# An attention and two mixture layers under one static order: longer planner costs for three kinds of VectorE and GpSimd steps, and an undivided early load of the first expert's w1

## The chip, the cores and the metric

The kernel runs on one core of a Trainium2 chip. The metric is the time of an execution in device microseconds (us), the median of several runs. TensorE (PE), VectorE (DVE), ScalarE (ACT), GpSimd (POOL) and SyncE (SP, which issues most DMAs) each run their own queue of instructions in order.

## The reference, cut to what matters

```python
# attention: q, k, v (4, 8, 576, 64), f (4, 8, 576)
scores = scale * (q @ k.T) + cum[:, :, :, None] - cum[:, :, None, :]   # causal mask
x = softmax(scores) @ v                                                # -> (2304, 512)
# dense layer, w_in (512, 2048), w_out (2048, 512)
h = maximum(x @ w_in, 0)
x = h * h @ w_out
# routed layer: 8 experts with 288 tokens each, taken in order of the logits
logits = x @ w_gate
for idx in argsort(-logits.flatten()):
    tok, e = idx // 8, idx % 8
    if assigned[tok] < 0 and counts[e] < 288:
        assigned[tok] = e; counts[e] += 1
for e in range(8):
    out[assigned == e] = maximum(x[assigned == e] @ w1[e], 0) @ w2[e]
```

`w_in` and `w_out` arrive as 64-bit floats.

## The kernel before, in words

**Attention** (`pair`, `attention`, `att_tail`) goes over 4 batches with 4 head pairs each, 16 pairs in all. Per pair TensorE makes score products in four query blocks (L501). VectorE adds the decay row and takes the row's extremum in one step (L518, tile `st`), ScalarE takes the exponential (L525), TensorE transposes (L557), ScalarE or VectorE evict (L385, L389), and TensorE multiplies with v (L574). Before a block's scores are reduced, the causal mask is added into its decay row (L513, VectorE or GpSimd). `norm_rows` (L604 to L616) inverts the sums, `norm` (L623) scales the output, which goes to DRAM (`xd`).

**Conversion** (`w_piece`, L653 to L657): each of 32 pieces of `w_in` and `w_out` comes as pairs of 32-bit words. Three VectorE steps make a 32-bit float `a`, then ScalarE or GpSimd round it to `hi`, and VectorE or GpSimd subtract (`lo`, L657).

**Dense layer**: chunks of 256 tokens (`moe1_x`, `moe1_up`, `moe1_down`). An up block is 12 products (L693 to L695: hi*hi, lo*hi, hi*lo), followed by ReLU, square, `hh` and `hl` (L710); a down block is three products (L717 to L719). `x2_rows` stores results to DRAM (`x2d`). On VectorE `gate_weights` (L850, L853) folds `w_out` with the gate matrix, and `x2_sums` (L798) makes logits of four chunks. Both read `wgb`, the gate matrix broadcast to all partitions, whose space is free only when attention is over.

**Routing and experts**: `phase(m)` finds by histograms which expert fills next and who its tokens are; `expert(m)` loads the expert's number into a register of SyncE (L1192), loads w1 and w2 with it (L1204, L1218), gathers tokens from `x2d` (`xg`, L1185), transposes (L1252), multiplies (L1272 or L1276 to L1278, L1301 or L1304 to L1306), and scatters (L1324). Experts 0 to 4 take their weights unsplit, 5 to 7 split into hi and lo. The weights lie in the slots `z0` to `z31` of the dense weights, most of which also hold the last two chunks' `h` tiles (`h2`).

**The order** is a plan. Each step is recorded with the engines that can do it and a cost in ns for each (`s.op({"dve": ..., "pool": ...}, ...)`), and with tiles it reads and writes. `Sched.run` plays these costs through a list schedule: whenever an engine is free, it takes the ready step of the least priority number for which slots are free, which also decides on which engine a step runs and which slot a tile gets. `emit` writes the queues in that order. Nothing of it is decided on the chip. `dve1(n)` is 70 + 1.04 n, `ptt(n)` 150 + 2.1 n. Priorities (`s.base`) are 0 to 2 for attention, 1 for conversion, 3 to 9 for the dense chunks, 12 for gate weights.

For the first expert the loads are written so:

```python
loads[i](0, 1 if 0 in HV else 2, after=self.x2_done if WX <= i else None)
```

`HV` is `[0]`, so each piece of w1 is loaded as two halves: first halves of pieces 0 and 1 as soon as the number is known, of 2 and 3 after the last stores to `x2d` (`x2_done`), and all second halves later, ordered after the first gather.

Of the kernel before, what the change touches and what calls it, by code (L numbers as in the profile page):

```python
# [32 lines left out]
RS = [("z", z) for z in (31, 30, 29)]  # L33
WS = [("z", 28)]
TM = 1
WX = 2
P0 = None
HV = [0]
NSM = 4
# [331 lines left out]
class K:  # L371
# [83 lines left out]
    def pair(self, b, pr):  # L455
# [35 lines left out]
        def scores(parts):  # L491

            sc = [s.buf(self.ps, [128, 512], F, "sc", 2, also=[("u", 0), ("u", 1)] if b < XB1 else []) for _ in range(2)]

            def f(e):
                o = 0
                for i, a, c in parts:
                    q0, n = QS[i]
                    for x in range(2):
                        hs = slice(64 * x, 64 * x + 64)  # L500
                        e.matmul(sc[x][:n, o:o + c - a], qr[hs, q0:q0 + n], kr[hs, a:c], start=True, stop=True)  # L501
                    o += c - a
            s.op({"pe": mm2(*[c - a for _, a, c in parts])}, f, r=[qr, kr], w=sc)
            done = []
            o = 0
            for i, a, c in parts:
                q0, n = QS[i]
                w = q0 + n
                if i not in live:
                    live[i] = [s.buf(ao, [128, S], F, "p", 3, also=X("p")) for _ in range(2)], [s.buf(ao, [128, 6], F, "st", 6) for _ in range(2)]  # L510
                    for x in range(2):

                        s.op({"dve": dve1(n), "pool": ptt(n)}, lambda e, row=rows[x], q0=q0, n=n, w=w: e.tensor_tensor(  # L513
                            row[:n, q0:w], self.maskb[:n, :n], row[:n, q0:w], op=OP.add), r=[self.maskb], w=[rows[x]])
                p, st = live[i]
                si = 1 if a else 0
                for x in range(2):
                    s.op({"dve": dve1(c - a) + 85}, lambda e, sc=sc[x], o=o, n=n, a=a, c=c, si=si, p=p[x], st=st[x], row=rows[x]: e.tensor_tensor_reduce(  # L518
                        out=p[:n, a:c], in0=sc[:n, o:o + c - a], in1=row[:n, a:c], scale=-0.125,
                        scalar=st[:n, si - 1:si] if si else 3e38, op0=OP.add, op1=OP.min,  # L520
                        accum_out=st[:n, si:si + 1]), r=[sc[x], rows[x]], w=[(p[x], si), st[x]])
                o += c - a
                if c == w:
                    for x in range(2):
                        s.op({"act": act(w, extra=2)}, lambda e, x=x, si=si, i=i, n=n, w=w, p=p[x], st=st[x]: e.activation(  # L525
                            p[:n, :w], p[:n, :w], AF.Exp, bias=st[:n, si:si + 1], scale=-1.0, accum_out=sums[:n, 5 * x + i:5 * x + i + 1]),
                            r=[st[x]], w=[p[x], (sums, (x, i))])
                    done.append((i, p))
            return done
# [71 lines left out]

    def norm_rows(self, b, pr, sums):
        s = self.s
        s.op({"dve": 75.0}, lambda e: e.tensor_scalar(sums.t, sums.t, 1e-9, None, op0=OP.add), w=[sums])  # L604
        s.op({"dve": 131.0}, lambda e: e.reciprocal(sums.t, sums.t), w=[sums])
        pt = s.buf(self.ps, [128, 4, 128], F, "pt", 1)
        s.op({"pe": 107.0}, lambda e: e.transpose(pt[:10, 0, :], sums.t, self.ident.t), r=[sums, self.ident], w=[pt])
        rt = s.buf(self.ao, [128, 128], F, "nrt", 2)
        s.op({"act": act(128, True), "dve": dve1(128)}, lambda e: self.rnd(e, rt[:10], pt[:10, 0, :]), r=[pt], w=[rt])
        self.dma(lambda: self.rd[b, pr], lambda: rt[:10], 5120, r=[rt], w=[(self.rd, (b, pr))])  # L610
        rbc = s.buf(self.mp, [128, S], F, "rbc", 0, also=[("wraw", 0), ("wraw", 1)])
        for j in range(2):
            for c0, c1, o in ((0, 64, 0), (64, S, 128)):
                self.dma(lambda j=j, c0=c0, c1=c1: rbc[64 * j:64 * j + 64, c0:c1],
                         lambda j=j, c0=c0, c1=c1, o=o: self.rd[b, pr, 5 * j:5 * j + 5].rearrange("i c -> (i c)")[None, o:o + c1 - c0].to_broadcast([64, c1 - c0]),
                         64 * (c1 - c0) * 4, r=[(self.rd, (b, pr))], w=[(rbc, (j, c0))])  # L616
        return rbc

    def norm(self, b, pr, rbc, xo):
        s = self.s  # L620
        for g, (c0, c1) in enumerate([(0, 320), (320, S)]):
            n = c1 - c0
            s.op({"dve": dve1(n), "pool": ptt(n)}, lambda e, c0=c0, c1=c1: e.tensor_mul(xo[:, c0:c1], xo[:, c0:c1], rbc[:, c0:c1]), r=[rbc], w=[(xo, g)])  # L623
        self.dma(lambda: self.xd[b, pr], lambda: xo.t, 128 * S * 4, r=[xo], w=[(self.xd, (b, pr))])

    def moe1_weights(self):
# [14 lines left out]
    def w_piece(self, which, r, c, half, raws, was, hold):  # L641
        s = self.s
        n = 512 if half is None else 256
        o = 256 * half if half else 0
        t, x = self.unit(which, r, c), r % 2
        bh, bl = self.wu[t]
        hi, lo = (lambda: bh[:, x, o:o + n]), (lambda: bl[:, x, o:o + n])
        src = (self.w_in, self.w_out)[which][r * 128:(r + 1) * 128, 512 * c + o:512 * c + o + n]
        raw = s.buf(self.mp, [128, n, 2], U32, "wraw", 0, also=raws)
        a = s.buf(self.mp, [128, n], U32, "wa", 1, also=was)  # L650
        self.dma(lambda: raw.t.rearrange("p a b -> p (a b)"), lambda: src.bitcast(U32), 128 * n * 8, w=[raw], after=hold)

        s.op({"dve": 60 + .52 * n}, lambda e: e.tensor_scalar(a.t, raw[:, :, 1], 3, 0x3FFFFFFF, op0=OP.logical_shift_left, op1=OP.bitwise_and), r=[raw], w=[a])  # L653
        s.op({"dve": dve1(n)}, lambda e: e.scalar_tensor_tensor(a.t, raw[:, :, 0], 29, a.t, op0=OP.logical_shift_right, op1=OP.bitwise_or), r=[raw], w=[a])
        s.op({"dve": dve1(n)}, lambda e: e.scalar_tensor_tensor(a.t, raw[:, :, 1], 0xC0000000, a.t, op0=OP.bitwise_and, op1=OP.bitwise_or), r=[raw], w=[a])
        s.op(hi_alts(n, WHI), lambda e: self.rnd(e, hi(), a.t.bitcast(F)), r=[a], w=[(bh, x)])
        s.op(lo_alts(n, WLO), lambda e: e.tensor_sub(lo(), a.t.bitcast(F), hi().bitcast(F)), r=[a, (bh, x)], w=[(bl, x)])  # L657

    def moe1_x(self, b, c, two=False):

# [515 lines left out]
    def expert(self, m, idx, widx):  # L1176
# [58 lines left out]
        else:  # L1235
            loads = [wload(0, i) for i in range(4)]
            for i in range(4):
                loads[i](0, 1 if 0 in HV else 2, after=self.x2_done if WX <= i else None)
            s.base = X0
            gather_x()  # L1240
            s.base = 30 + m
            if 0 in HV:
                for i in range(4):
                    loads[i](1, 2, hold=True)
            for i in range(4):
                wload(1, i)(0, 2, hold=True)
        s.base = (XB + m if m else X0)
# [188 lines left out]
```

## Time and profile before

| | |
|---|---|
| median of 3 runs | 995.26 us (993.12 to 998.85) |
| the profiled execution's own time | 997.44 us |
| its span | 995.7 us |
| busy: PE, DVE, ACT, POOL | 929.3, 637.0, 392.1, 344.9 us |
| mean granted clock of TensorE | 0.972 |

The span runs from the first to the last instruction. A matmul's duration contains its pipeline's length, so a busy TensorE can still have room; idle TensorE is time in which no matmul was under way. Idle time of an engine that isn't the bound costs nothing.

### The profile page before, as it was taken

What the parts mean: (1) busy time and instruction counts of PE and PEld (TensorE: products, weight loads), DVE (VectorE), ACT (ScalarE), POOL (GpSimd) and SP (SyncE); (2) the same over time, 40 slices, a digit from 0 to 9 for tenths busy, and PEclk for the clock granted to TensorE, in tenths of its full rate; (3) what the DMA queues carried; (4) which work ended last, traced back from release to release, by engine and by line L of the source; (5) the groups of instructions that cost most, each with busy time, mean ns of one, the idle gap of its engine ahead of it and who ended that gap; (6) DMA issues with size and microseconds to landing.
All of it is one profiled execution on the core that took longest, in us unless ns stands there. A gap on an engine that the chain in (4) does not pass through costs nothing. (4 is left out here: it accounts for less than half of the span.)

```text
span 995.7 us, 17474 instructions
## 1 busy us (share of the span) xinstructions
PE 929.3 (93%) x6135; PEld 749.8 (75%) x6135; DVE 637.0 (64%) x2037; ACT 392.1 (39%) x1068; POOL 344.9 (35%) x459
## 2 busy tenths in 40 slices
PE   6897899899999999999999999994999979999996
PEld 3554455677779898989989899774777867778995
DVE  6999888984438999992627322576767786422231
ACT  4665567655634444444343366200101021224320
POOL 2555555653333425341313100001113050557921
PEclk9999899999999999999999999996999998999998
DMA  6668677642230101010100000007735450334410
GB/s 215 206 222 266 197 238 248 194 136 85 75 129 24 44 1 43 1 44 1 43 15 9 22 1 2 11 33 214 241 134 201 176 175 22 111 110 151 133 48 24
DMA packets 48615, 105.66 MB, mean 106 GB/s; under 512 B 10280, under 2 KB 18632, under 8 KB 48400
## 3 DMA queue, kind: packets, MB, share of 16 engines
q1 hardware_dynamic: 45456, 95.11, 29.0%
q0 software_dynamic: 3072, 9.44, 3.2%
q8 instruction: 48, 0.79, 0.3%
q14 instruction: 39, 0.32, 0.1%
HBM read 90.20 MB, written 14.33 MB: 105 GB/s over the span
## 5 line engine op out<-in xcount | busy, mean ns | idle before, releaser
L693 PE MATMUL u<-xh,z 128*128 128x256 f32 x512 | 147.6, 288 | 2.4 <-ACT r L698 1.9
L694 PE MATMUL u<-xh,z 128*128 128x256 f32 x512 | 144.8, 283 | 0.0
L695 PE MATMUL u<-xl,z 128*128 128x256 f32 x512 | 144.7, 283 | 0.0
L698 ACT ACTIVATE r<-u 128x256 f32<-128x256 f32 x144 | 54.6, 380 | 162.7 <-PE u L695 138.0
L710 POOL TENSOR_TENSOR hl<-r,hh 128x256 fp32r<-128x256 f32 x79 | 74.7, 947 | 117.4 <-ACT hh L385 100.7
L853 DVE CUSTOM_DVE_ANT_0 gjk<-wof,wgb 128x512 bf16<-128x512 f32 x128 | 108.1, 845 | 11.0 <-DMA wgb<-wgT 8.0
L693 PEld LDWEIGHTS u<-xh,z 128*128 128x128 f32 x512 | 97.2, 190 | 15.3 <-issue 3.1
L694 PEld LDWEIGHTS u<-xh,z 128*128 128x128 f32 x512 | 97.4, 190 | 8.0
L695 PEld LDWEIGHTS u<-xl,z 128*128 128x128 f32 x512 | 97.3, 190 | 0.0
L1301 PE MATMUL acc<-ehh,z 128*128 128x288 f32 x320 | 91.8, 420 | 0.0
L719 PE MATMUL acc<-z,hl 128*128 128x512 f32 x224 | 88.6, 396 | 2.9 <-POOL hl L710 2.1
L717 PE MATMUL acc<-z,hh 128*128 128x512 f32 x224 | 90.1, 402 | 0.0
L718 PE MATMUL acc<-z,hh 128*128 128x512 f32 x224 | 89.2, 398 | 0.0
L1272 PE MATMUL u<-exh,z 128*128 128x288 f32 x304 | 87.0, 422 | 0.1
L1224 POOL TENSOR_TENSOR z<-wr,z 128x512 fp32r<-128x512 f32 x48 | 61.3, 1312 | 48.1 <-ACT z L385 48.0
L525 ACT ACTIVATE p<-p,st 128x448 f32<-128x448 f32 (+4 forms) x109 | 59.9, 550 | 37.7 <-DVE st L518 37.4
L513 POOL TENSOR_TENSOR row<-maskb,row 128x128 f32<-128x128 bf16 (+1 forms) x90 | 45.8, 516 | 69.0 <-DVE st L518 48.4
L1301 PEld LDWEIGHTS acc<-ehh,z 128*128 128x128 f32 x320 | 57.5, 194 | 16.3 <-issue 2.0
L1272 PEld LDWEIGHTS u<-exh,z 128*128 128x128 f32 x304 | 55.8, 195 | 14.8 <-DVE exh L389 0.3
L1185 POOL DMA_INDIRECT xg<-x2d,ph_idx x24 | 25.6, 1065 | 99.4 <-DVE ph_P L1127 51.9
L699 ACT ACTIVATE r<-r 128x256 f32<-128x256 f32 x139 | 58.0, 418 | 4.2
L1324 POOL DMA_INDIRECT out_dram<-yo,ph_idx x24 | 24.3, 1011 | 100.8 <-DVE ph_q L1034 32.7
(354 smaller groups left out, 2199.2 us busy)
## 6 DMA issues: line engine op xcount, KB each, us to landing
z<-in_w_dram SPq DMA_DIRECT2D x36, 512.0 KB
wr<-in_w_dram SPq DMA_DIRECT2D x24, 512.0 KB
z<-in_w_in_dram SPq DMA_DIRECT2D x16, 512.0 KB
z<-in_w_out_dram SPq DMA_DIRECT2D x14, 512.0 KB
row<-cumd SPq DMA_DIRECT2D x24, 288.0 KB
xd<-xo SPq DMA_DIRECT2D x16, 288.0 KB
wraw<-rd SPq DMA_DIRECT2D x32, 128.0 KB
xa<-xd SPq DMA_DIRECT2D x8, 512.0 KB
```

What stands on the lines that cost most here:

```text
L525: s.op({"act": act(w, extra=2)}, lambda e, x=x, si=si, i=i, n=n, w=w, p=p[x], st=st[x]: e.activation(p[:n, :w], p[:n, :w], AF.Exp, bias=st ...
L693: e.matmul(u[:, :256], wh[:, k % 2, fs], xh[k][1](), start=(k == 0), stop=False)
L694: e.matmul(u[:, :256], wl[:, k % 2, fs], xh[k][1](), start=False, stop=False)
L695: e.matmul(u[:, :256], wh[:, k % 2, fs], xl[k][1](), start=False, stop=(k == 3))
L710: s.op(lo_alts(256), lambda e: e.tensor_sub(hl(), r.t, hh().bitcast(F)), r=[r, kh], w=[kl])
L717: g = [lambda e: e.matmul(acc.t, hh()[:, ts], wh[:, f % 2], start=(f == 0), stop=False), lambda e: e.matmul(acc.t, hh()[:, ts], wl[:, f % ...
L718: lambda e: e.matmul(acc.t, hh()[:, ts], wl[:, f % 2], start=False, stop=False),
L719: lambda e: e.matmul(acc.t, hl()[:, ts], wh[:, f % 2], start=False, stop=(f == 15))]
L853: s.op({"dve": dve1(DM) + 85}, lambda e, f=f, x=x, wo=wo, jk=jk: e.tensor_tensor_reduce(out=jk.t, in0=wo.t, in1=wb[:, x, :], scale=1.0, sc ...
L1224: s.op(lo_alts(512, LOE(m, which, i, 0, c)), lambda e, cs=cs: e.tensor_sub(lo[:, cs], raw[:, cs], hi[:, cs].bitcast(F)), r=[(raw, key), (h ...
L1272: s.op({"pe": 1.69 * CAP}, lambda e, k=k: e.matmul(u[:, :CAP], whi[0][k][:, fs], xh[k].t, start=(k == 0), stop=(k == 3)), r=[(whi[0][k], c ...
L1301: e.matmul(acc[:, :CAP], wh[:, ds], hh.t, start=(f == 0), stop=(f == 7))
```

## The change

Costs of the plan are raised: the mask's add by 180 ns (VectorE) and 130 (GpSimd), the add to the sums from 75 to 340 ns, the norm's product by 200 on both, the three conversion steps from 326, 602, 602 to 592, 652, 652 ns at 512 columns, and the conversion's `lo` by 300 (VectorE) and 100 (GpSimd). No instruction of these steps is another. The first expert's w1 is loaded in four whole pieces, all as soon as the number is known.

```diff
@@ -33,7 +33,6 @@
 RS = [("z", z) for z in (31, 30, 29)]
 WS = [("z", 28)]
 TM = 1
-WX = 2
 P0 = None
 HV = [0]
 NSM = 4
@@ -510,7 +509,7 @@
                     live[i] = [s.buf(ao, [128, S], F, "p", 3, also=X("p")) for _ in range(2)], [s.buf(ao, [128, 6], F, "st", 6) for _ in range(2)]
                     for x in range(2):
 
-                        s.op({"dve": dve1(n), "pool": ptt(n)}, lambda e, row=rows[x], q0=q0, n=n, w=w: e.tensor_tensor(
+                        s.op({"dve": dve1(n) + 180, "pool": ptt(n) + 130}, lambda e, row=rows[x], q0=q0, n=n, w=w: e.tensor_tensor(
                             row[:n, q0:w], self.maskb[:n, :n], row[:n, q0:w], op=OP.add), r=[self.maskb], w=[rows[x]])
                 p, st = live[i]
                 si = 1 if a else 0
@@ -601,7 +600,7 @@
 
     def norm_rows(self, b, pr, sums):
         s = self.s
-        s.op({"dve": 75.0}, lambda e: e.tensor_scalar(sums.t, sums.t, 1e-9, None, op0=OP.add), w=[sums])
+        s.op({"dve": 340.0}, lambda e: e.tensor_scalar(sums.t, sums.t, 1e-9, None, op0=OP.add), w=[sums])
         s.op({"dve": 131.0}, lambda e: e.reciprocal(sums.t, sums.t), w=[sums])
         pt = s.buf(self.ps, [128, 4, 128], F, "pt", 1)
         s.op({"pe": 107.0}, lambda e: e.transpose(pt[:10, 0, :], sums.t, self.ident.t), r=[sums, self.ident], w=[pt])
@@ -620,7 +619,7 @@
         s = self.s
         for g, (c0, c1) in enumerate([(0, 320), (320, S)]):
             n = c1 - c0
-            s.op({"dve": dve1(n), "pool": ptt(n)}, lambda e, c0=c0, c1=c1: e.tensor_mul(xo[:, c0:c1], xo[:, c0:c1], rbc[:, c0:c1]), r=[rbc], w=[(xo, g)])
+            s.op({"dve": dve1(n) + 200, "pool": ptt(n) + 200}, lambda e, c0=c0, c1=c1: e.tensor_mul(xo[:, c0:c1], xo[:, c0:c1], rbc[:, c0:c1]), r=[rbc], w=[(xo, g)])
         self.dma(lambda: self.xd[b, pr], lambda: xo.t, 128 * S * 4, r=[xo], w=[(self.xd, (b, pr))])
 
     def moe1_weights(self):
@@ -650,11 +649,11 @@
         a = s.buf(self.mp, [128, n], U32, "wa", 1, also=was)
         self.dma(lambda: raw.t.rearrange("p a b -> p (a b)"), lambda: src.bitcast(U32), 128 * n * 8, w=[raw], after=hold)
 
-        s.op({"dve": 60 + .52 * n}, lambda e: e.tensor_scalar(a.t, raw[:, :, 1], 3, 0x3FFFFFFF, op0=OP.logical_shift_left, op1=OP.bitwise_and), r=[raw], w=[a])
-        s.op({"dve": dve1(n)}, lambda e: e.scalar_tensor_tensor(a.t, raw[:, :, 0], 29, a.t, op0=OP.logical_shift_right, op1=OP.bitwise_or), r=[raw], w=[a])
-        s.op({"dve": dve1(n)}, lambda e: e.scalar_tensor_tensor(a.t, raw[:, :, 1], 0xC0000000, a.t, op0=OP.bitwise_and, op1=OP.bitwise_or), r=[raw], w=[a])
+        s.op({"dve": 80 + n}, lambda e: e.tensor_scalar(a.t, raw[:, :, 1], 3, 0x3FFFFFFF, op0=OP.logical_shift_left, op1=OP.bitwise_and), r=[raw], w=[a])
+        s.op({"dve": dve1(n) + 50}, lambda e: e.scalar_tensor_tensor(a.t, raw[:, :, 0], 29, a.t, op0=OP.logical_shift_right, op1=OP.bitwise_or), r=[raw], w=[a])
+        s.op({"dve": dve1(n) + 50}, lambda e: e.scalar_tensor_tensor(a.t, raw[:, :, 1], 0xC0000000, a.t, op0=OP.bitwise_and, op1=OP.bitwise_or), r=[raw], w=[a])
         s.op(hi_alts(n, WHI), lambda e: self.rnd(e, hi(), a.t.bitcast(F)), r=[a], w=[(bh, x)])
-        s.op(lo_alts(n, WLO), lambda e: e.tensor_sub(lo(), a.t.bitcast(F), hi().bitcast(F)), r=[a, (bh, x)], w=[(bl, x)])
+        s.op({"dve": dve1(n) + 300, "pool": ptt(n) + 100}, lambda e: e.tensor_sub(lo(), a.t.bitcast(F), hi().bitcast(F)), r=[a, (bh, x)], w=[(bl, x)])
 
     def moe1_x(self, b, c, two=False):
 
@@ -1235,13 +1234,10 @@
         else:
             loads = [wload(0, i) for i in range(4)]
             for i in range(4):
-                loads[i](0, 1 if 0 in HV else 2, after=self.x2_done if WX <= i else None)
+                loads[i](0, 2)
             s.base = X0
             gather_x()
             s.base = 30 + m
-            if 0 in HV:
-                for i in range(4):
-                    loads[i](1, 2, hold=True)
             for i in range(4):
                 wload(1, i)(0, 2, hold=True)
         s.base = (XB + m if m else X0)
```

On TensorE, in attention, these are the instructions around the first up product (`u<-xh`) of the dense layer: before, 676 instructions come ahead of it, in the 13th pair. `sc`, `pt`, `ov`, `acc` and `u` are PSUM banks.

```order
L557 MATMUL acc_2369<-ident,z_2292 128x128 x4
L557 MATMUL ov_2384<-ident,z_2271 128x128
L557 MATMUL ov_2384<-ident,z_2292 128x128
L693 MATMUL u_2390<-xh_1231,z_310 128x256
L694 MATMUL u_2390<-xh_1231,z_340 128x256
L695 MATMUL u_2390<-xl_1256,z_310 128x256
L693 MATMUL u_2390<-xh_1236,z_310 128x256
```

In the changed kernel (its line numbers are one less) 499 instructions come ahead of it, in the 10th pair:

```order
L500 MATMUL sc_1787<-z_1184,z_1171 64x64
L500 MATMUL sc_1788<-z_1184,z_1171 64x64
L692 MATMUL u_1799<-xh_1202,z_317 128x256
L693 MATMUL u_1799<-xh_1202,z_333 128x256
L694 MATMUL u_1799<-xl_1231,z_317 128x256
L556 MATMUL pt_1807<-ident,p_1752 128x128 x4
L556 MATMUL acc_1808<-ident,p_1770 128x128 x4
L692 MATMUL u_1799<-xh_1206,z_317 128x256
L693 MATMUL u_1799<-xh_1206,z_333 128x256
```

The up block moved from behind the 12th pair's products to the middle of the 10th's scores and transposes.

On VectorE, after attention, around the first `hl` of the dense layer, before: 120 lines of gate work (`gjk`, `gf` and `wof`; a product has two lines) stand ahead of it.

```order
L853 ISA gf_3936 128x1
L853 ISA gjk_4545,gf_3936<-wof_4390,wgb_3845 128x512
L853 ISA gf_3936 128x1
L710 TENSOR_TENSOR hl_4555<-r_4539,hh_4550 128x256
L853 ISA gjk_4557,gf_3936<-wof_4481,wgb_3845 128x512
L853 ISA gf_3936 128x1
```

The same place in the changed kernel, with 69 such lines ahead:

```order
L852 ISA gf_4105 128x1
L852 ISA gjk_4462,gf_4105<-wof_4319,wgb_4016 128x512
L852 ISA gf_4105 128x1
L709 TENSOR_TENSOR hl_4472<-r_4456,hh_4467 128x256
L852 ISA gjk_4474,gf_4105<-wof_4395,wgb_4016 128x512
L852 ISA gf_4105 128x1
```

The first `hl` on VectorE now stands behind fewer gate products.

On SyncE, at the end of the dense layer: `x2d` are the last stores of tokens, `ph_ei` the load of the expert's number, the DMAs from `in_w` w1. Before:

```order
L392 DMA x2d<-wraw_7797 128x512
L1192 TENSOR_LOAD ph_ei_7890
L1192 ISA x2
L1204 ISA
L1204 DMA z_7910<-in_w_dram 128x512
L1204 ISA
L1204 DMA z_7918<-in_w_dram 128x512
L392 DMA x2d<-wraw_7926 128x512
L392 DMA x2d<-wraw_8159 64x512 x2
L392 DMA x2d<-wraw_8226 64x512 x2
L1204 ISA
L1204 DMA z_8238<-in_w_dram 128x512
```

Changed:

```order
L1191 TENSOR_LOAD ph_ei_7890
L1191 ISA x2
L1203 ISA
L1203 DMA z_7910<-in_w_dram 128x1024
L1203 ISA
L1203 DMA z_7918<-in_w_dram 128x1024
L1203 ISA
L1203 DMA z_7925<-in_w_dram 128x1024
L1203 ISA
L1203 DMA z_7934<-in_w_dram 128x1024
L391 DMA x2d<-wraw_7928 128x512
L391 DMA x2d<-wraw_8163 64x512 x2
```

Four loads of 128 x 1024 stand together ahead of the last stores, in place of two of 128 x 512 ahead and two behind; the next load of a number follows the stores at once.

## Rows read from the trace of the kernel before

**Rows 1.** The page, its first line.
```profile
span 995.7 us, 17474 instructions
```

**Rows 2.** Busy time by stage: stretch, its length, engines with counts, PEclk, DMA share, GB/s.
```profile
0.00:180.00 180.00, 154.48 (x1024) 89.83 (x1025) 156.75 (x520) 110.75 (x347) 93.41 (x165) 0.94 0.69 225
300.00:450.00 150.00, 146.96 (x934) 131.36 (x934) 143.96 (x340) 67.31 (x168) 60.34 (x64) 1.00 0.07 22
450.00:650.00 200.00, 199.21 (x1364) 179.25 (x1363) 81.42 (x228) 85.75 (x217) 26.80 (x35) 1.00 0.04 13
650.00:700.00 50.00, 37.31 (x239) 29.63 (x238) 35.54 (x175) 1.93 (x4) 6.79 (x6) 0.80 0.49 148
800.00:996.00 196.00, 177.38 (x1151) 154.99 (x1149) 76.34 (x243) 49.19 (x107) 93.56 (x101) 0.97 0.31 98
```

**Rows 3.** Waits of TensorE, 0 to 200 us: total us, times, longest.
```profile
PE sc L501 <- DVE st L518: 10.9, 6, 4.1
PE u L693 <- ACT r L698: 1.9, 1, 1.9
```

**Rows 4.** Groups of VectorE, 0 to 210 us: busy us, mean ns, idle before.
```profile
L389 DVE COPY pa<-acc 128x384 f32<-128x384 f32 x7 | 3.7, 544 | 0.1
L389 DVE COPY pb<-pt 128x128 f32<-128x128 f32 x9 | 2.2, 276 | 0.0
```

**Rows 5.** Lines L653 and L657, 0 to 300 us: ns min/median/max, starts, forms.
```profile
L653 DVE TENSOR_SCALAR z<-z x14: 406/420/5066, 22.8 to 196.1; 128x512 uint32<-128x512 uint32 x14
L657 POOL TENSOR_TENSOR z<-wa,z x16: 726/1270/1332, 25.4 to 222.9; 128x512 fp32r<-128x512 f32 x12, 128x256 fp32r<-128x256 f32 x4
L657 DVE TENSOR_TENSOR z<-z,z x5: 885/916/1796, 75.3 to 200.5; 128x512 fp32r<-128x512 f32 x5
```

**Rows 6.** Timeline near 92 us: start, duration in us, engine, line, operation [idle before].
```profile
92.06 5.07 DVE L653 TENSOR_SCALAR z<-z 128x512 uint32<-128x512 uint32 x1
95.44 1.40 POOL L680 TENSOR_TENSOR xl<-xa,xh 128x256 fp32r<-128x256 f32 x2
97.91 0.47 PE L501 MATMUL sc<-qk,qk 64*128 64x64 f32 x1 [4.13 <-DVE st L518]
```

**Rows 7.** Timeline of TensorE, dense stretch: one up product, two down products.
```profile
500.94 0.28 PE L695 MATMUL u<-xl,z 128*128 128x256 f32 x1
501.06 0.40 PE L717 MATMUL acc<-z,hh 128*128 128x512 f32 x1
501.29 0.40 PE L718 MATMUL acc<-z,hh 128*128 128x512 f32 x1
```

**Rows 8.** Busy time of one stretch of attention.
```profile
130.00:180.00 50.00, 47.27 (x355) 28.93 (x354) 45.74 (x162) 35.09 (x113) 28.31 (x47) 1.00 0.73 233
```

**Rows 9.** Timeline of TensorE and VectorE: attention's end, first gate product, a wait.
```profile
284.47 1.56 PE L574 MATMUL ov<-pa,vr 64*64 64x320 f32 x12
301.18 0.69 DVE L853 CUSTOM_DVE_ANT_0 gjk<-wof,wgb 128x512 bf16<-128x512 f32 x1 [8.01 <-DMA wgb<-wgT]
428.73 0.50 PE L719 MATMUL acc<-z,hl 128*128 128x512 f32 x1 [0.53 <-DVE hl L710]
```

**Rows 10.** Timelines at the first expert: SyncE, GpSimd, TensorE, ScalarE.
```profile
652.72 0.97 SPq L1204 DMA_DIRECT2D z<-in_w_dram  x2
678.96 102.15 SPq L1204 DMA_DIRECT2D z<-in_w_dram  x42
684.89 0.92 POOL L1185 DMA_INDIRECT xg<-x2d,ph_idx  x1 [0.30 <-issue]
691.18 0.42 PE L1252 MATMUL pt<-ident,xg 96*128 96x96 f32 x1 [6.30 <-DMA xg<-x2d,ph_idx]
696.06 0.41 ACT L385 ACTIVATE exh<-acc 128x288 f32<-128x288 f32 x1
696.10 6.29 PE L1272 MATMUL u<-exh,z 128*128 128x288 f32 x16
```

**Rows 11.** Chain of waits, last stage: start us, us, what.
```profile
929.43 3.15 DMA xg<-x2d,ph_idx
```

## The prediction

> **What bounds the kernel now.** I read the span first, then the stages, then inside each stage the wait that ends last. The profiled execution took 997.44 us by its own time, 995.7 us of it the span [rows 1]; the median of the three runs shown, 995.26 us, lies 2.2 us under it. In the stage table [rows 2] TensorE's column (the second) says where time can be had. From 300 to 650 us TensorE is busy 346.2 of 350 us: only less TensorE work would help there, and the change touches none. Idle TensorE is found in three places: 25.5 us in the first 180 us, 12.7 us between 650 and 700, 18.6 us after 800. In the first stage VectorE is busy 156.8 of 180 us, the nearest thing to a bound, and TensorE's largest wait is for VectorE's score reduction `st` (10.9 us, with 4.1 us the longest) [rows 3]. The granted clock is 0.94 of full in this stage and 1.00 in the dense stretch [rows 2].
>
> So the time is: start of the dense stretch, plus work of TensorE that doesn't change, plus the route's bubble, plus the last experts. An edit of planner costs can only act where the two orders differ. On TensorE they differ up to place 1545 (about 331 us) and again from place 4805 (the last three experts); between them the orders are the same but for some 30 rows. That is where I look.
>
> **Part 1, VectorE relief in attention.** With its longer steps the planner gives VectorE less. Ahead of the reductions of the 13th head pair (some 176 us) the changed order has 17 evictions fewer on VectorE (81 to 64), mostly of 128 to 512 columns, two `lo` subtractions fewer and one norm more. Rows of such evictions are 276 and 544 ns [rows 4]; over the mix I take 0.34 us, 5.8 us in all. Two `lo` at 0.9 us give 1.8 us [rows 5]; the extra norm and two small masks take back some 0.6 us. Sum: 7.0 us less on VectorE. Ahead of the ninth pair it is 10.3 us, because three conversions of three steps also move behind it. How much arrives? VectorE is busy 87% of the stage [rows 2], so 6.1 us if the bound is as it looks. Ends: 0 (another chain binds) and 10.3.
>
> The work isn't gone. GpSimd gets some 6 us more ahead of the 13th pair (two `lo` at 1.27 us [rows 5], five `hl` of early products, less a little) and ScalarE some 14, a part of it the early products' squares and roundings; ScalarE is busy 110.8 of 180 us and GpSimd 93.4 [rows 2], so that both have room as a sum.
>
> A row speaks against counting it as free. A conversion step of VectorE that takes 420 ns in the median once took 5066 [rows 5]: it began at 92.06 us, while GpSimd ran one elementwise step after another until 96.84 us, and the score product waited 4.13 us behind it [rows 6]. The Trainium skill, page "SBUF — State Buffer", section "SBUF: two separate sides", says that VectorE (in a two-port mode, or with two SBUF inputs against a GpSimd operation that reads SBUF) and GpSimd lock each other out of one port pair for a whole instruction. The trace agrees in that one row; were every added microsecond of GpSimd paid so, the 6.1 us would shrink to nothing. I don't take it in full, since the typical rows stay near their shortest (420 of at least 406 ns) [rows 5]; it is a rival below.
>
> **Part 2, fillers.** Before, TensorE's first up product of the dense layer stood behind 676 instructions; now behind 499, within the tenth pair. In pairs 9 to 11 (counted from 0) stand 60 up products and 21 down products that came later before. At a pitch of 0.12 and 0.23 us [rows 7] that is 7.2 + 4.8 = 12.0 us of TensorE's work moved into a stretch that waits for others. Free is what fits into gaps: 130 to 180 us shows 50 - 47.27 = 2.7 us of idle [rows 8]. I take 2.7; ends 0 and 12.0, since short pauses inside chained products don't show as idle.
>
> **Part 3, the clock.** Fewer stalls mean fewer slices at the lower of the two levels (1.2 against 2.4 GHz). A mean of 0.94 over 180 us [rows 2] is 10.8 us lost as an upper bound. I take 1.5 us. Front, together: 6.1 + 2.7 + 1.5 = 10.3 us gained; ends 0 and 19.
>
> **Part 4, what is late next.** The fillers push attention's last product back in TensorE's order, from place 1262 to 1390. The broadcast gate matrix `wgb` can only be loaded after attention, and 368 lines of gate work on VectorE hang on it. Before: last attention product at 284.47, first gate product at 301.18, 16.7 us later; VectorE is then busy 144.0 of the 150 us to 450 [rows 2, 9]. Place 2139, a down product, started at 428.73 after waiting 0.53 us for VectorE's `hl` [rows 9]. So 877 places took 144.3 us, 0.1645 us each, and 128 places are 21.1 us. Now, with the front's gain g: last attention product at 284.5 + 21.1 - g, first gate product at 322.3 - g. Ahead of the `hl` for place 2139 now stand 237 gate lines instead of 284, at 127.1 us / 284 = 0.447 us each (from 301.18 to the `hl` before 428.73 [rows 9]) that is 106.0 us, and three more `hl` and three more `xl` (0.4 and 0.9 us) add 3.9. The `hl` comes at 432.2 - g, TensorE wants it at 428.2 - g: a wait of about 4 us whatever g is; I take 3.8. Ends 0 (the gate load comes sooner after attention) and 8. This wait I expect as a cluster before downs between about 370 and 440 us.
>
> **Part 5, w1 of the first expert.** Its four pieces of 512 KB now go out with the first two, at about 652.7 us [rows 10], in a queue that is otherwise empty, instead of six later issues (two half pieces behind x2d's last stores, four behind the second expert's w1). What TensorE waited for there was not w1: it stood 6.30 us until gathered rows came (691.18), and the up products began at 696.10, 0.04 us after the last operand copy began at 696.06 [rows 10], with no wait for a weight. So the load's removal is hidden: 0. What could help is a gather with less traffic beside it: the same landing in the last stage took 3.15 us [rows 11], against 691.18 less 685.81 (the end of the third gather's issue, 684.89 + 0.92) = 5.4 [rows 10], at most 2.2 us. But the second expert's w1 and w2 follow in the queue at once, so I take 0.5. The cost: x2d's stores are queued behind four loads, the last of which waits for a slot (`z16`) that the first chunk's last down product frees. Place 3371 stands close to the stores' own data, and the critical store is 18 us later: 0, at worst 1. The last experts are reordered without a reason that I can price; 18.6 us of idle there [rows 2] bound it, I take 0 with 4 us either way.
>
> **Sum:** -10.3 + 3.8 - 0.5 = -7.0 us. Against the profiled execution's own 997.44 us that gives 990.4, against the median 988.3 us, which I forecast. Some 0.5% (5 us) is what a measurement can tell from no change. Its own range: 980 to 993.
>
> **Rivals.**
> *GpSimd takes the relief back.* By the row of 5.07 us [rows 6] and the page's rule, 6.1 us of VectorE relief and the clock's 1.5 are lost, fillers stay: -2.7 + 3.8 - 0.5 = +0.6, 995.9 us. For it: masks on GpSimd wait and block as well, and more stand there now. Against: the medians [rows 5].
> *Slower: fillers stall in order.* For the first three batches the score products alternate over four PSUM banks, two of them the up products' own. An up product in pairs 9 to 11 takes one away and waits for it; the one time that an up product waited for ScalarE's `r` it cost 1.9 us [rows 3]. Five blocks of 12 up products at 1.9 us are 9.4 us, the fillers' 2.7 and the clock's 1.5 don't come: -6.1 + 9.4 + 3.8 - 0.5 = +6.6, 1001.9 us. With w us per block the sum is 5 w - 2.8: it takes the gain away from 0.6 us per block on and is slower by over 0.5% from 1.6.
> *Fillers wholly free.* Then 12.0 in place of 2.7 and VectorE's 10.3 in full: -12.0 - 8.0 + 3.8 - 0.5, with 8.0 between 6.1 and 10.3, = -16.7, 978.6 us. For it: TensorE's weight loads are busy only half the first stage (89.8 of 180 us) [rows 2], against 131.4 of 150 later.
> *No change:* that the orders don't differ is excluded, they do on every engine.
>
> **Chances.** Forecast 0.52, GpSimd 0.22, slower 0.15, free fillers 0.11. Of the forecast's share about 0.10 ends within 5 us of 995.3, of the GpSimd rival's 0.02 above it. Faster 0.42 + 0.11 = 0.53, same 0.10 + 0.20 = 0.30, slower 0.17. The range 979 to 1000 leaves out the tail of free fillers and most of the slow case.
>
> **What would show it.** Right: VectorE busy less and GpSimd more before 180 us; TensorE's wait for `st` under 8 us; up products from about 145 us on; last attention product near 295 to 300 us; first gate product near 312; TensorE waits for `hl` of a few us between 370 and 440; first expert's w1 in one run near 653 us and its up products starting no sooner after the gather. Wrong: single VectorE steps of several us beside GpSimd (first rival), waits at the first up products in pairs 9 to 11 (second), no wait for `hl` and a gain over 12 us (third), or a difference made after 800 us, on which I have no forecast.

## The result, and the profile of the changed kernel

The changed kernel takes 982.68 us (median of 6 runs, 977.44 to 985.2) against 995.67 us before (6 runs, 993.12 to 998.85): a ratio of 0.9854, 95% interval 0.983 to 0.9878. That is 13.0 us less, where 7.0 were forecast; the time lies in the range 979 to 1000. The profiled execution took 982.32 us, 980.5 of it the span, 15.1 us less than the profiled one of before (997.44); 2.1 of these are the spread of single executions. Ratios, here and below, leave out executions over 1.5% above the fastest of their kernel (among them one of lo_only, 1044.5 us at a granted clock of 0.838, and one of order_only, 996.33 us), while the medians in us are of all.

The stages of the changed kernel, with the stretches of [rows 2] and the one between (columns: stretch, length, busy us and instructions of PE, PEld, DVE, ACT, POOL, PEclk, DMA share, GB/s):

```profile
0.00:180.00 180.00, 159.42 (x1038) 93.96 (x1039) 140.42 (x484) 113.76 (x352) 91.88 (x163) 0.94 0.68 219
180.00:300.00 120.00, 119.12 (x837) 88.67 (x836) 78.95 (x220) 71.98 (x218) 59.98 (x89) 1.00 0.37 113
300.00:450.00 150.00, 148.12 (x942) 132.59 (x941) 136.84 (x330) 67.10 (x166) 53.85 (x60) 1.00 0.12 40
450.00:650.00 200.00, 199.21 (x1356) 177.65 (x1355) 95.33 (x292) 82.38 (x209) 30.68 (x38) 1.00 0.07 23
800.00:996.00 196.00, 166.11 (x1075) 146.53 (x1073) 67.65 (x194) 46.93 (x102) 87.58 (x93) 0.97 0.28 89
```

TensorE's idle time in the first 180 us falls from 25.5 to 20.6 us, and from 180 to 300 us from 5.0 to 0.9. The kernel before, from 180 to 300 us:

```profile
180.00:300.00 120.00, 115.02 (x789) 86.21 (x789) 71.87 (x207) 65.30 (x199) 51.34 (x77) 0.99 0.38 126
```

VectorE is busy 140.4 us in the first stage in place of 156.8. GpSimd is busy 91.9 in place of 93.4: the relief did not go to it. The waits of TensorE up to 200 us answer to [rows 3] (us in total, times, longest):

```profile
PE sc L500 <- DVE st L517: 4.3, 5, 1.6
PE pt L556 <- ACT p L524: 3.4, 4, 1.6
PE pt L606 <- ACT pa L384: 1.9, 2, 1.7
```

The wait for `st` falls from 10.9 to 4.3 us, and no up product waits for `r`. Most of that fall lies ahead of 131 us, where no up product stands yet, since the first one starts at 132.03 us. From 0 to 131 us, before and then changed:

```profile
PE sc L501 <- DVE st L518: 9.7, 4, 4.1
```

```profile
PE sc L500 <- DVE st L517: 4.0, 4, 1.6
```

The timeline at the end of attention, at the gate stage and at the first gather answers to [rows 9, 10]:

```profile
295.57 0.76 PE L573 MATMUL ov<-pa,vr 64*64 64x320 f32 x4
...
310.43 0.69 DVE L852 CUSTOM_DVE_ANT_0 gjk<-wof,wgb 128x512 bf16<-128x512 f32 x1 [7.45 <-DMA wgb<-wgT]
...
417.20 0.88 DVE L709 TENSOR_TENSOR hl<-r,hh 128x256 fp32r<-128x256 f32 x1
...
418.13 0.50 PE L718 MATMUL acc<-z,hl 128*128 128x512 f32 x1 [0.18 <-DVE hl L709]
...
642.07 2.11 SPq L1203 DMA_DIRECT2D z<-in_w_dram  x4
...
678.59 0.42 PE L1248 MATMUL pt<-ident,xg 96*128 96x96 f32 x1 [4.35 <-DMA xg<-x2d,ph_idx]
```

Set one under the other, the two traces say where the time came from. The last up product of the dense layer, before and in the changed kernel:

```profile
626.91 0.28 PE L695 MATMUL u<-xa,z 128*128 128x256 f32 x1
```

```profile
616.26 0.28 PE L694 MATMUL u<-xa,z 128*128 128x256 f32 x1
```

The difference has been 10.6 us since 430 us without a change (428.73 against 418.13 for the product that waits for `hl`): all of it is earned ahead of that. At the first expert's gather it becomes 12.6 (678.59 against 691.18), at the end of the span 15.2.

### The profile page after: what moved, and what is told of

Read it like the earlier page. It is cut to its first block, busy times and chain, and to the rows that moved or that the text cites. A ratio compares the mean times of both kernels' runs of the same rounds, so it can differ in the third digit from the quotient of the medians.

```text
span 980.5 us, 17456 instructions
## 1 busy us (share of the span) xinstructions
PE 930.0 (95%) x6135; PEld 748.6 (76%) x6135; DVE 625.1 (64%) x2015; ACT 396.9 (40%) x1079; POOL 349.2 (36%) x470
## 5 line engine op out<-in xcount | busy, mean ns | idle before, releaser
L852 DVE CUSTOM_DVE_ANT_0 gjk<-wof,wgb 128x512 bf16<-128x512 f32 x128 | 104.7, 818 | 9.9 <-DMA wgb<-wgT 7.4
L512 POOL TENSOR_TENSOR row<-maskb,row 128x128 f32<-128x128 bf16 (+1 forms) x97 | 47.9, 498 | 64.7 <-DVE st L517 36.6
```

The costliest lines, as they stand in the source:

```text
L852: s.op({"dve": dve1(DM) + 85}, lambda e, f=f, x=x, wo=wo, jk=jk: e.tensor_tensor_reduce(out=jk.t, in0=wo.t, in1=wb[:, x, :], scale=1.0, sc ...
```

## The experiments

First the change is taken apart. Each ratio is against executions of the kernel before on the same chip, whose medians lie between 996.7 and 999.6 us. The recorded ranges in us start from 995.3, so they are read by the gain that they stand for.

**costs_only** keeps the new costs and puts back the loading of w1 (the last hunk of the diff and `WX` undone).

> The changed costs with the loads of w1 as before. The order differs from before only up to about 331 us, and from there on it is that of before. In the two profiles the changed kernel gained 10.6 us up to 430 us, kept them unchanged to 622 us, 2.0 more at the first expert's gather and 2.5 more in the last experts. Theory (the parts add up): 10.6 of the 15.2 us of span, scaled to the medians' 13.0 us a gain of about 9, 986 to 987 us. Rival (the front's gain is lost at the next wait unless w1 comes early): a gain under 4 us, above 991.

Measured: 980.26 us, ratio 0.9853 (0.9792 to 0.9914). The costs give all of the gain. The last up product:

```profile
615.85 0.28 PE L695 MATMUL u<-xa,z 128*128 128x256 f32 x1
```

**w1_only** has the costs of before and the new loading.

> The costs as before, w1 of the first expert in whole early pieces. The order is that of before up to the end of the dense layer. Theory (the parts add up): gather wait 4.3 us in place of 6.3, and the last experts as in the changed kernel, together a gain of 4 us, about 991 to 992; the 5.07 us VectorE step at 92 us comes again. My prediction's term for this part was 0.5 us (ends 0 and 2.2) plus 0 for the last experts: 995. Rival (measured differences of this size are the spread of runs): 995 to 996.

Measured: 994.99 us, ratio 0.9993 (0.9963 to 1.0022): nothing. The long VectorE step and TensorE's wait came again at the same place:

```profile
91.97 5.06 DVE L653 TENSOR_SCALAR z<-z 128x512 uint32<-128x512 uint32 x1
...
97.81 0.43 PE L501 MATMUL sc<-qk,qk 64*128 64x64 f32 x1 [4.13 <-DVE st L518]
...
691.33 0.42 PE L1249 MATMUL pt<-ident,xg 96*128 96x96 f32 x1 [4.72 <-DMA xg<-x2d,ph_idx]
```

The gather did come sooner here (4.72 us of wait, before 6.30 [rows 10]), yet so it did in costs_only with the old loading (4.9 us). From the first gathered transposition to the end of the span pass 304.5 us before, 302.4 in w1_only, 301.4 in costs_only and 301.9 in the changed kernel; costs_only has the order of before there, and so has fillers_held below, with 309.0. The 4.5 us that the pair of traces showed behind 650 us are therefore the spread of single executions, not the work of the change.

**conv_only** raises only the costs of the conversion, **lo_only** only that of `lo`:

```diff
-        s.op({"dve": 60 + .52 * n}, lambda e: e.tensor_scalar(a.t, ...
+        s.op({"dve": 80 + n}, lambda e: e.tensor_scalar(a.t, ...
...
-        s.op(lo_alts(n, WLO), lambda e: e.tensor_sub(lo(), ...
+        s.op({"dve": dve1(n) + 300, "pool": ptt(n) + 100}, lambda e: e.tensor_sub(lo(), ...
```

> Only the costs of the conversion (three steps and lo) are raised. Its order has as little VectorE work ahead of the 13th pair as the changed kernel (9.4 us less than before by the rows' medians, the changed kernel 6.6), but no early fillers: the first up product stands behind 684 TensorE instructions (before 676, changed 499). Theory of the prediction (VectorE relief is the main term): the last attention product some 6 to 8 us earlier and a total near 988 to 990. Rival (the fillers carry the gain): no gain, 994 to 996.

> Only the cost of lo is raised. The counterpart: fillers early (first up product behind 499 instructions, as in the changed kernel), but VectorE relieved by 1.6 us only ahead of the 13th pair. Theory of the prediction: 1.4 us of relief and 2.7 of fillers, and fewer stalls no more than before: 991 to 993. Rival (the fillers carry the gain): 986 to 988. A third way (any other order moves the time by several us either way): above 996.

Measured: 993.5 us, ratio 0.9974 (0.9941 to 1.0006), and 993.71 us, 0.9973 (0.9936 to 1.0009). Neither VectorE's relief without early fillers nor early fillers with little relief gives more than a few us. For conv_only the theory (988 to 990) is wrong and the rival nearer; for lo_only the rival (986 to 988) is wrong and the theory at its edge.

The next ones separate the order from the engines, and one long step from both. **engines_only** keeps the order of before and takes each step's engine from the plan of costs_only, **order_only** the reverse. After the plan is made and before the queues are written:

```diff
     order = s.run()
+    for e, seqs in ENG.items():
+        for q in seqs:
+            s.tasks[q].eng = e
```

> The order of before on TensorE (but for seven places), and every step on the engine that the raised costs give it: 194 steps change their engine, VectorE has 6.6 us less work ahead of the 13th pair (178.3 in place of 184.9 by the medians of rows). The two kernels with one half of the costs gave no gain worth the name (ratios 0.997), so that the parts don't act alone as my prediction had them. Theory A (Part 1 of the prediction, VectorE's relief carries the front): last attention product some 6 us earlier, 989 to 991. Theory B (the order of TensorE's instructions carries it): 994 to 998. Theory C (each is worth about half of the 13): 988 to 991 here and the same in the counterpart.

> The counterpart: the order that the raised costs give, every step on the engine that it had before; VectorE has 184.1 us ahead of the 13th pair as before (184.9), the first up product stands behind 499 instructions as in the changed kernel. Theory A (relief): 990 to 994. Theory B (order): 981 to 985. Theory C (each half): 988 to 991.

Measured: 1005.94 us, ratio 1.0088 (1.0055 to 1.012), and 987.61 us, 0.9875 (0.9836 to 0.9914). A lighter VectorE under the old order made the kernel slower than any of the theories had it; the new order on the old engines keeps most of the gain, as theory B (order) has it. VectorE is busy 148.08 us of the first 180 there (before 156.75), and TensorE waits longer:

```profile
PE sc L506 <- DVE st L523: 12.0, 9, 2.4
...
PE pt L612 <- ACT pa L390: 4.5, 4, 2.2
```

The steps that changed their engine stand in the other engine's queue where the old order has them, and TensorE waits for ScalarE's `pa`. The pair tells that the relief by itself isn't the cause, and that the order gives most of the gain without it; it does not price it exactly, since each hybrid also carries an order that was laid out for other engines.

**one_step_moved** is the kernel before with one L653 step eight steps further down VectorE's queue:

```diff
     order = s.run()
+    dve = [x for x in order if x.eng == "dve"]
+    i = dve.index([x for x in dve if x.fn.__code__.co_firstlineno == 653][11])
+    order.remove(dve[i])
+    order.insert(order.index(dve[i + 8]) + 1, dve[i])
```

> The kernel before with a single VectorE instruction eight steps further down its queue: the conversion step that took 5.07 us beside GpSimd's burst in the profile of before and, with the same 4.12 us of TensorE wait, in that of w1_only. Theory (the long step is held by GpSimd's instructions and TensorE pays for it): the step takes about 0.4 us at its new place or is held for the rest of the burst only, the 4.1 us wait at 98 us goes, 991 to 992. Rival (the next wait for VectorE, 2.5 us at 120 us, takes it back): 994 to 996. If the instruction is held as long at its new place, the burst isn't the cause.

Measured: 994.44 us, ratio 0.9966 (0.9943 to 0.9988), 3.4 us less, the gain that the theory stands for. At its new place, beside the end of GpSimd's burst, the step took 0.67 us:

```profile
97.68 0.66 PE L557 MATMUL ov<-ident,p 128*128 128x128 f32 x4 [2.40 <-ACT pb L385]
...
98.92 1.42 POOL L680 TENSOR_TENSOR xl<-xa,xh 128x256 fp32r<-128x256 f32 x2
99.95 0.67 DVE L653 TENSOR_SCALAR z<-z 128x512 uint32<-128x512 uint32 x1
```

The wait of 4.13 us for `st` is gone, and at nearly the same time stands one of 2.40 us for ScalarE's `pb`. So the one held step is about a quarter of the 13 us, by the interval 1.2 to 5.7; in the profile the last up product starts only 0.8 us earlier than before (626.13).

**masks_norm_only** raises the other costs: mask, add to the sums, norm.

> Only the costs of the mask, of the add to the sums and of the norm's product are raised: both features of the changed kernel, early fillers (first up product behind 434 instructions) and VectorE relieved by 6.1 us ahead of the 13th pair. If relief and fillers together are what it takes, 984 to 987; if any order other than the changed kernel's falls back, 993 to 997.

Measured: 994.59 us, ratio 0.9972 (0.9948 to 0.9996): relief and some fillers together are not enough. The two halves of the costs, conv_only and masks_norm_only, give 0.26% and 0.28%, together they give 1.5%: the costs don't act one by one.

The last ones test the fillers, through the plan. **fillers_held** is costs_only with a dependency more:

```diff
+    k.upt[0].deps.add(k.sct[48])
+    k.sct[48].succ.append(k.upt[0])
     order = s.run()
```

(`upt` lists the up products' steps, `sct` those of the score products, four to a head pair.)

> The kernel of costs_only with one thing more: in the plan, the first up product of the dense layer may not start before the first score product of the 13th pair. TensorE's order is that of costs_only for the first 499 instructions (about 131 us) and again from about place 1572; between them the fillers are gone (last attention product at place 1252 in place of 1390, before 1262), while VectorE has even less ahead of the 13th pair (174.0 us, costs_only 178.3, before 184.9). Theory F (dense products that run in attention's pauses carry the front; engines_only has ruled out that a lighter VectorE does it alone): most of the gain goes, 989 to 994. Theory R (the first 131 us and the engines carry it, the 5.07 us step being absent): 980 to 985. Half and half: 986 to 988.

Measured: 998.35 us, ratio 1.003 (1.0 to 1.0059). The whole gain goes, more than any of the theories had it, and the last up product starts as late as before (626.91):

```profile
626.83 0.28 PE L696 MATMUL u<-xa,z 128*128 128x256 f32 x1
```

Up to 131 us the two kernels have the same order on TensorE; behind it they part. By stretches, first costs_only, then fillers_held, each from 0 to 131 and from 131 to 200 us, and last the first stretch of before:

```profile
0.00:131.00 131.00, 113.72 (x730) 63.80 (x730) 101.91 (x365) 83.35 (x257) 64.11 (x122) 0.95 0.70 225
131.00:200.00 69.00, 65.61 (x454) 43.92 (x452) 52.99 (x158) 43.32 (x137) 38.06 (x59) 0.95 0.61 193
```

```profile
0.00:131.00 131.00, 112.55 (x734) 63.80 (x734) 102.78 (x365) 84.41 (x258) 64.99 (x123) 0.97 0.71 225
131.00:200.00 69.00, 60.73 (x412) 38.62 (x410) 61.53 (x180) 45.76 (x143) 41.52 (x58) 0.93 0.67 216
```

```profile
0.00:131.00 131.00, 108.21 (x679) 61.34 (x679) 111.95 (x361) 76.53 (x240) 66.07 (x120) 0.92 0.68 222
```

TensorE works 4.9 us less in the 69 us when the fillers are held, and the waits of that stretch show what for, in costs_only, then in fillers_held:

```profile
PE sc L501 <- DVE st L518: 0.4, 1, 0.4
```

```profile
PE sc L502 <- DVE st L519: 4.6, 2, 3.1
```

With the fillers held the score products wait 4.6 us for VectorE; with dense products between them TensorE comes to them later and waits 0.4. The granted clock there is 0.93 against 0.95.

The first 131 us show the other half: much is won there without any filler. The sums of the eighth pair, ahead of which no dense product stands in these kernels, are transposed 8 us sooner; before, the changed kernel and fillers_held:

```profile
133.88 0.28 PE L607 MATMUL pt<-ident,sums 128*10 128x128 f32 x1
```

```profile
126.10 0.27 PE L606 MATMUL pt<-ident,sums 128*10 128x128 f32 x1
```

```profile
125.40 0.27 PE L608 MATMUL pt<-ident,sums 128*10 128x128 f32 x1
```

This lead is not VectorE's relief either: lo_only, relieved by 1.6 us, has it (125.78 us), conv_only, relieved by 9.4 us, hasn't (134.74). With the fillers it is kept: attention's last product comes 11.1 us later than before (295.57 against 284.47) behind 120 more dense products, by the pitches of [rows 7] an estimated 18.7 us of work, so 7.6 us of the lead of 7.8 are left. Without fillers the waits that follow take it back.

**sums_400** and **costs_105** are costs_only with slightly other numbers (the add to the sums 400 for 340; mask 189 and 136, sums 353, norm 210, `lo` 315 and 105).

> The kernel of costs_only with one number changed again, the add to the sums 400 ns in place of 340. The plan is another from place 217 on: first up product behind 358 instructions, last attention product at place 1420 (costs_only 1390, before 1262), VectorE relieved by 3.3 us only ahead of the 13th pair (181.6). Theory F (fillers): as good as costs_only, 979 to 984. Theory R (relief, early stretch): 987 to 992. Theory L (a plan is a lottery ticket, no feature tells): anywhere between 984 and 1000.

> The kernel of costs_only with its added costs some 5% larger (mask 189 and 136, sums 353, norm 210, lo 315 and 105). The plan is another from place 267 on: first up product behind 676 instructions as before the change, last attention product at place 1306 (before 1262, costs_only 1390), VectorE relieved by 16.6 us ahead of the 13th pair (168.3), the most of all. Theory F (fillers): 44 of 128 places, 990 to 994. Theory R (relief): 979 to 985. A theory by which nearly true costs are what counts and not the single order: as costs_only, 979 to 984.

Measured: 984.96 us, ratio 0.9885 (0.9844 to 0.9927), and 985.67 us, 0.9884 (0.985 to 0.9917). The first stands just above the fillers' range (979 to 984). The second is against it: with only 36 dense products more than before it has nearly the same gain, in its trace 6.1 us of it ahead of the last up product. By its gain it fits the theory of relief as well as that of nearly true costs.

**costs_doubled** doubles every raise.

> The kernel of costs_only with every raise of the change doubled (mask 360 and 260, sums 605, norm 400, conversion steps at 512 columns 858, 702, 702, lo 600 and 200), so that the plan's costs lie far above the durations of the rows. By its features the order is as good as that of costs_only: 291 up and 135 down products ahead of the last attention product, the same as there (before 210 and 96), and VectorE has less ahead of the 13th pair (172.4 us, costs_only 178.3). Three kernels with costs near the rows' durations (costs_only, sums_400, costs_105) gained 11 to 15 us with quite different features. Theory T (costs near the rows' durations are what the order needs, on either side an instruction waits where the plan says it doesn't or the plan leaves room that isn't needed): 989 to 995. Theory E (raised costs make room on VectorE, how true they are is no matter; features decide): 979 to 985.

Measured: 989.52 us against 999.61 on that chip, ratio 0.9897 (0.9877 to 0.9918). In us it stands in the first theory's range, but beside the before of its own chip it gains 10.1 us, nearly what sums_400 and costs_105 do. That costs must lie near the true durations is not borne out: twice the raise still helps.

The runs in one table. "Dense" counts up and down products in TensorE's queue ahead of attention's last product; "VectorE" is its work ahead of the 13th pair's reductions, by the order and the median durations of the trace of before; "idle" is TensorE's idle time in the first 450 us, "last up" is when the dense layer's last up product starts, both in the profile.

| | dense | VectorE, us | idle, us | last up, us | ratio |
|---|---|---|---|---|---|
| before | 306 | 184.9 | 33.5 | 626.91 | |
| conv_only | 297 | 175.5 | 31.8 | 627.59 | 0.9974 |
| fillers_held | 300 | 174.0 | 31.4 | 626.83 | 1.003 |
| engines_only | 307 | 178.3 | 36.2 | 636.46 | 1.0088 |
| masks_norm_only | 324 | 178.8 | 33.6 | 626.75 | 0.9972 |
| costs_105 | 342 | 168.3 | 28.3 | 620.78 | 0.9884 |
| lo_only | 384 | 183.3 | 30.1 | 625.08 | 0.9973 |
| changed | 426 | 178.3 | 23.3 | 616.26 | 0.9854 |
| costs_only | 426 | 178.3 | 23.2 | 615.85 | 0.9853 |
| order_only | 426 | 184.1 | 27.1 | 627.22 | 0.9875 |
| costs_doubled | 426 | 172.4 | 26.7 | 617.79 | 0.9897 |
| sums_400 | 456 | 181.6 | 27.1 | 617.49 | 0.9885 |

Idle time and last up are each from one execution. That of order_only took 996.33 us, 8.7 over its median, so its 627.22 says little; that of costs_doubled took 982.02 us, 7.5 under its own. The other kernels with 426 or more dense products win 9 to 11 us by the last up product, those with 324 or fewer win none, whatever VectorE is spared. Between them neither of the first two columns sorts: lo_only has 78 more and wins 1.8 us, costs_105 has 36 more and wins 6.1. The idle time does sort: it is 23.2 to 28.3 us in every kernel that gains 1% or more, and 30.1 or more in every other. So what is won is TensorE's waiting ahead of 450 us; this is the gain in another form, though, and doesn't tell which feature of an order saves it.

## Why the prediction was right, and which of its steps weren't

The sign, the range and the place were right: faster, ahead of 331 us, by the planner's other order. Of the marks named, the wait for `st` is 4.3 us (under 8 forecast), the last attention product stands at 295.57 (295 to 300), the first gate product at 310.43 (near 312), w1 goes out in one run of 2.11 us. Up products start at 132.03 us (145 forecast). Two marks did not come: GpSimd is not busier ahead of 180 us, and TensorE has no wait of a few us for `hl`. The time lies in the forecast case's own range too (980 to 993). But the gain is nearly twice the sum (13.0 for 7.0 us), and the front came out near its 10.3 us by terms that missed in both directions, which is luck.

**Part 1, VectorE relief, 6.1 us: the step that failed.** It took work saved on the busiest engine for time saved on TensorE. engines_only saves the same work and is 0.9% slower; conv_only and fillers_held save 9.4 and 10.9 us and are no further at the last up product. The lead of 7.8 us at the eighth pair comes with the order, in lo_only nearly without relief. Only costs_105, with the largest relief and few fillers, leaves it a share.

**Part 2, fillers, 2.7 us of 0 to 12.** Here it was decided whether the gain stays. The 2.7 us came from the idle time of one window, 130 to 180 us of the kernel before [rows 8]. But fillers don't only fill gaps that the old trace shows: their 18.7 us (an estimate, above) cost attention next to nothing, since its lead is 7.8 us at the eighth pair and 7.6 at the end. Holding them costs 11.0 us at the last up product (626.83 in fillers_held, 615.85 in costs_only), inside the upper end of 12.0. That they are needed in this plan is shown; that they are enough is not (lo_only).

**Part 3, clock, 1.5 us.** Between the two traces the size fits: ahead of 300 us TensorE stands at the lower level for 23.8 us before and 20.4 in the changed kernel, all the difference behind 180 us (granted clock 1.00 in place of 0.99), and at 1.2 in place of 2.4 GHz those 3.4 us cost 1.7 at most. But the changed kernel's profiled execution has the lowest clock of its six (0.973). Over all executions the mean granted clock has a median of 0.972 before and of 0.978 to 0.982 in changed, costs_only, order_only, sums_400 and costs_105, while all kernels without a gain of 1% lie at 0.970 to 0.975 (costs_doubled has 0.974, where before has 0.969 on its chip). Whether that is a cause of the gain or follows from fewer waits no run separates. w1_only speaks for a small price: with the order of before its clock is lower in the first 180 us, 0.91 in place of 0.94, and its last up product starts 1.7 us later (628.63).

```profile
0.00:180.00 180.00, 155.53 (x1010) 88.80 (x1011) 155.15 (x515) 110.04 (x342) 89.91 (x163) 0.91 0.70 224
```

**Front, 10.3 us.** As a sum it holds: 10.6 us at 430 us. By the prediction's own count (128 places, 21.1 us) the last attention product came 284.47 + 21.1 - 295.57 = 10.0 us sooner; by the pitches of its own Part 2 it is the 7.6 us above, and the rest is won between there and 430 us.

**Part 4, the wait for `hl`, +3.8 us: the term that made the forecast too long.** It was a difference of two large numbers (432.2 - 428.2 = 4.0, entered as 3.8). The `hl` was forecast for 432.2 - 10.0 = 422.2 us and ended at 417.20 + 0.88 = 418.08: the first gate product came 14.9 us after attention's last in place of 16.7, and the way from it to the `hl` took 107.6 us in place of 109.9. TensorE, forecast there at 418.2, waited 0.18 us. An error of 3% in VectorE's path was the whole term; the low end, 0, was right.

**Part 5.** w1's 0 is borne out by w1_only (interval -0.4% to +0.2%). The gather's 0.5 us can't be told from spread: its wait is 4.35 us now and 4.72 in w1_only, and 4.9 in costs_only with the old loading. The last experts' 0, with 4 us either way, is what the runs show too.

**The rivals.** GpSimd did not take the relief back: it is busy 1.5 us less in the first stage, and no wait of TensorE for `st` is over 1.6 us. Up products that stall in order did not come. Of the third, wholly free fillers (978.6 us), both marks came, no wait for `hl` and a gain over 12 us, and the time lies between it and the forecast; its reason, that the fillers cost nothing, is what the traces show between the eighth pair and attention's end.

**Open:** what gives the lead ahead of the eighth pair, which feature of the order makes lo_only win so little and costs_105 so much, and what share the clock has. The runs exclude relief alone and one long step alone as the whole cause, and true costs as a condition; they don't give a rule by which the count of fillers foretells the time.

## What to carry to other kernels

In a planned order, price a change of costs by what the waiting engine does in its waits, not by the work that the busiest engine is spared: hold the filler work back in one run, and see whether the gain goes. Where a forecast wait is the difference of two paths of a hundred us, take it as zero with its ends, since an error of 3% in one of them was the whole term here. And before two traces are read against each other, measure how far two executions of the same order differ in each stage: here 1.7 us up to 430 us (440.4 and 442.1 for the same product in before and w1_only) and several us behind the gather, which looked like an effect and was none.

## What the hardware showed that wasn't expected

A VectorE step of 0.42 us can be held through seven GpSimd instructions in a row. In two programs with the same order ahead of it the step at 92 us took 5.07 and 5.06 us, from within the first to just behind the last instruction of GpSimd's burst (91.97 to 97.03 in w1_only, whose timeline this is):

```profile
91.47 0.74 POOL L513 TENSOR_TENSOR z<-maskb,z 64x64 f32<-64x64 bf16 x1
92.17 0.71 POOL L680 TENSOR_TENSOR xl<-xa,xh 128x256 fp32r<-128x256 f32 x1
92.86 0.61 POOL L387 TENSOR_SCALAR z<-wa 128x512 fp32r<-128x512 f32 x1
93.44 0.71 POOL L680 TENSOR_TENSOR xl<-xa,xh 128x256 fp32r<-128x256 f32 x1
94.12 1.25 POOL L657 TENSOR_TENSOR z<-wa,z 128x512 fp32r<-128x512 f32 x1
95.34 1.40 POOL L680 TENSOR_TENSOR xl<-xa,xh 128x256 fp32r<-128x256 f32 x2
```

The Trainium skill, page "SBUF — State Buffer", section "SBUF: two separate sides", says that of a GpSimd instruction and a VectorE step in a two-port mode or with two SBUF inputs (the latter against a GpSimd operation that reads SBUF) the one that starts first gets the shared ports for its whole instruction. By that sentence alone one would expect the step to be let in at the end of an instruction; these rows show that where GpSimd's queue has no pause it may not be. That these ports are what holds it is inferred from the times.

A burst doesn't always hold it. In the changed kernel a step of the same kind began beside one GpSimd instruction and ended 0.28 us behind the next (92.82 and 92.54), while a third ran:

```profile
91.11 0.73 POOL L512 TENSOR_TENSOR row<-maskb,row 64x64 f32<-64x64 bf16 x1
91.61 1.21 DVE L652 TENSOR_SCALAR wa<-z 128x512 uint32<-128x512 uint32 x1
91.82 0.72 POOL L679 TENSOR_TENSOR xl<-xa,xh 128x256 fp32r<-128x256 f32 x1
92.50 1.46 POOL L656 TENSOR_TENSOR z<-z,z 128x512 fp32r<-128x512 f32 x1
```

In one_step_moved the step began beside the burst's last instruction and also ended 0.28 us behind it (100.62 and 100.34), so its 0.67 us don't tell how it would have fared earlier in the burst. And the long hold is not the conversion's alone: in costs_105 a mask's add of 64 columns (median of this line 0.29 us) was held through six GpSimd instructions, the last of which ended at 95.88, and TensorE waited behind it. That kernel gains 1.2% all the same.

```profile
91.52 4.44 DVE L513 TENSOR_TENSOR row<-maskb,row 64x64 f32<-64x64 bf16 x1
...
96.62 0.86 PE L501 MATMUL sc<-qk,qk 64*128 64x64 f32 x4 [2.82 <-DVE st L518]
```
